# 64-row attention heads and a pipeline rotated by half a group in an attention-plus-FFN kernel

## The chip, the cores and the metric

The kernel runs on one core of one Trainium2 chip. The metric is the device time of one execution in microseconds (us), lower is better. A run has a state: slow when it is more than 1.5% above the fastest run of the same kernel, else fast; only fast runs are compared in ratios (a median is of all runs). The profile shows one execution. Its span is about 1.8 us shorter than the device time of the same execution (329.5 against 331.33 us), so profile spans and times are not mixed below.

Engines are named as the profile names them: PE is TensorE (matmul), PEld its weight loads, DVE VectorE, ACT ScalarE, POOL GpSimd, SP SyncE, which here only issues DMAs (SPq).

## The reference

There are 8 batches, 8 heads, 576 tokens and 64 columns per head. Every head gets two attentions that are added: a local one, in which token i sees the tokens with |i - j| < 4, and one over q, k and v averaged by fours (144 tokens), whose result is repeated four times. The sum becomes x with 4608 rows and 512 columns and goes through an FFN:

```python
def _attn_ref(q, k, v):                       # cut
    q_d = q.reshape(B, H, Sd, 4, D).mean(axis=3)      # k_d, v_d alike
    out_up = np.repeat(sm_attn(q_d, k_d, v_d), 4, axis=2)
    scores = np.where(np.abs(i - j) < 4, scale * q @ k.T, -1e9)
    return out_up + softmax(scores) @ v

def _moe_ref(x, w_in, w_out):
    h = x @ w_in                              # 512 -> 2048
    return (h * (1 / (1 + np.exp(-1.702 * h)))) @ w_out   # 2048 -> 512
```

## The kernel before

The FFN is cut into 9 groups of 512 tokens. A group is 64 large matmuls of the first product (16 blocks of 4, each followed by a silu on ACT) and 64 of the second. The attention of batch g + 1 is threaded into group g at fixed positions. A position below 16 counts blocks of the first product; from 16 on it counts single matmuls of the second.

```python
POS = [13, 16, 33, 42, 53, 62, 71]
# s_pe(0), s_act(0), scores of quad 1, values 0-1, values 2-3, transposes 0-1, 2-3

def prep_1(name, b, qd):                    # DVE: q or k of four heads, transposed
    store, dst = {"k": (kf, kT), "q": (qf, qT)}[name]
    tt = work.tile([128, S, 2], BF16, ...)
    nc.vector.transpose(out=..., in_=store[b, qd]...)   # pairs of bf16 moved as one fp32
    dst[b, qd] = tt

def scores(b, qd, barred=False):            # local scores of a quad of heads
    sp = [ps_tile(), ps_tile()]             # two of three PSUM tiles in rotation
    for i in range(5):
        for a in range(2):                  # even and odd columns of the head
            for par in range(2):
                for r in range(4):
                    rows = slice(32 * r, 32 * r + 32)
                    nc.tensor.matmul(sp[r // 2][...],
                        lhsT=kT[b, qd][rows, k0 : k0 + 64, a],
                        rhs=qT[b, qd][rows, q0 : q0 + 60, a],
                        start=(a == 0), stop=(a == 1),
                        tile_position=(32 * r, 64 * par))      # 80 matmuls
    return sp
# scores_d (pooled): the same way, 24 matmuls; pool_qk makes its operands on POOL

    for g in range(n_groups):               # cut
        ...
        elif b < B:                         # b = g + 1
            load_v4(b)                      # six DMAs on SP
            prep_qk(b, 0); pool_qk(b, 0)
            load_qk(b + 1, 0); load_qk(b + 1, 1)     # POOL's queue
            prep_v(b, nc.gpsimd)
            load_v(b + 1)                   # ten DMAs on SP
            prep_qk(b, 1); pool_qk(b, 1)
            prep_v4(b, nc.gpsimd)
```

The transpose moves pairs of bf16 numbers (in the trace one instruction of 128x576 f32, 1.24 us, the next 1.09 us later), so the 64 columns of a head lie on 32 partitions, with two columns behind each other on each. A head therefore takes two accumulating matmuls of 32 rows for every block of scores.

The softmax here doesn't subtract the row's maximum and nothing guards it: scores larger than these inputs give would overflow.

## Time and profile before

| | before |
|---|---|
| time, median of 3 | 329.24 us (328.62 to 329.56) |
| span of the profile | 329.5 us |
| TensorE busy | 308.0 us (93%) |
| groups 1 to 6, each with the attention of one batch | 33.4 to 35.1 us |
| groups 7 and 8, FFN alone | 27.6 and 31.4 us |

These lines are from the page of the kernel before: busy time of each engine (share of the span, instructions), and the shares of the chain that ended last, by engine.

```profile
PE 308.0 (93%) x4987; PEld 157.9 (48%) x5043; DVE 130.2 (40%) x215; ACT 184.1 (56%) x322; POOL 138.9 (42%) x168
...
PE 87%; issue 4%; SPq 3%; ACT 2%; DVE 2%; DMA 1%; DVEq 0%; ACTq 0%
```

TensorE is the limit: it is nearly always busy, and its work is 87% of the chain.

The next lines are the windows view, one line for a group, cut where the first large matmul of each group starts: groups 1, 2, 3, 6 and 7.

```profile
core 0: us, PE busy (x) PEld busy (x) DVE busy (x) ACT busy (x) POOL busy (x), PEclk, DMA share, GB/s
67.08:102.18 35.10, 33.30 (x594) 17.04 (x600) 17.43 (x27) 21.73 (x39) 17.52 (x19) 1.00 0.74 161
102.18:135.89 33.71, 32.80 (x594) 16.91 (x600) 16.34 (x25) 20.95 (x36) 17.52 (x19) 1.00 0.68 142
135.89:169.42 33.53, 32.63 (x594) 16.88 (x600) 16.33 (x25) 20.95 (x36) 17.53 (x19) 1.00 0.68 143
237.13:270.53 33.40, 32.50 (x595) 16.75 (x601) 14.99 (x25) 20.95 (x36) 15.25 (x15) 1.00 0.28 69
270.53:298.15 27.62, 27.51 (x127) 12.50 (x128) 0.52 (x2) 11.94 (x20) 0.00 (x0) 1.00 0.10 39
```

Group 7 has no attention: 27.62 us are 128 large matmuls. The attention of a batch costs TensorE the rest, 33.40 - 27.62 = 5.8 us. PEclk, the mean granted clock of TensorE, is 1.00 in every group. DVE works about half of a group, POOL too.

One block of scores stands like this in the timeline of TensorE (start, time until the end of the last one, line, names, shapes, count):

```profile
147.21 0.84 PE L351 MATMUL pa<-qT,kT 32*64 32x60 bf16 x80
147.85 0.59 PE L370 MATMUL pa<-qdT,kdT 32*64 32x144 bf16 x24
148.38 2.76 PE L618 MATMUL pm<-xT,w_in_bf 128*128 128x512 bf16 x11
```

The 80 local matmuls take 0.64 us until the pooled ones start, 8 ns each. So it is mostly their number that costs, and the change halves it.

### The profile page before, as it was taken

The numbers are of one execution on the slowest core, as the hardware profiler recorded it, in microseconds if no ns is written. First come the engines' busy times: TensorE is split into PE (matmuls) and PEld (weight loads), VectorE is DVE, ScalarE is ACT, GpSimd is POOL, SyncE is SP. The second block draws the span as 40 slices with busy tenths as digits, with TensorE's granted clock in tenths as the row PEclk, the third lists the DMA queues.
The fourth block names the chain that finished last, engine by engine and source line by source line (L and its number), as shares of the span: only waits on it lengthen the run. The fifth ranks groups of instructions, "written<-read, shape, count | busy, mean of one in ns | idle before, by whom it ended". The sixth has DMA issues, their size and how long they took to land.

```text
span 329.5 us, 11220 instructions
## 1 busy us (share of the span) xinstructions
PE 308.0 (93%) x4987; PEld 157.9 (48%) x5043; DVE 130.2 (40%) x215; ACT 184.1 (56%) x322; POOL 138.9 (42%) x168
## 2 busy tenths in 40 slices
PE   8767999789999999999999999998999999999995
PEld 3444455445554455455544555455444544444444
DVE  4870512770468036802771277225730560000000
ACT  2552773375936683667367746674566646415611
POOL 7890844049603970298029901990098000000000
PEclk9997999999999999999999999999999999999999
DMA  7999979999814991398339922993180110011011
GB/s 126 184 188 208 171 151 183 196 210 236 191 39 132 205 207 39 116 193 171 102 100 200 200 83 86 196 195 105 40 172 2 60 41 32 2 72 56 2 62 65
DMA packets 63552, 41.36 MB, mean 126 GB/s; under 512 B 44048, under 2 KB 54416, under 8 KB 63504
## 3 DMA queue, kind: packets, MB, share of 16 engines
q1 hardware_dynamic: 55056, 26.95, 35.8%
q0 software_dynamic: 8304, 13.63, 23.9%
q8 instruction: 39, 0.64, 0.9%
q14 instruction: 9, 0.07, 0.1%
q10 hardware_dynamic: 144, 0.07, 0.1%
HBM read 44.83 MB, written 9.44 MB: 165 GB/s over the span
## 4 chain that ended last, share of the span: by engine, by line
PE 87%; issue 4%; SPq 3%; ACT 2%; DVE 2%; DMA 1%; DVEq 0%; ACTq 0%
PE pm L618 35%; PE pm L674 33%; PE pa L351 3%; SPq L214 3%; PE pa L618 2%; PE pa L431 2%; PE pa L409 2%; PE pa L370 2%; PE pa L458 2%; PE pa L674 2%; DMA vf<-in_v_dram 1%; PE pm L689 1%; PE pa L484 1%; ACT vd L321 0%; PE pa L312 0%
## 5 line engine op out<-in xcount | busy, mean ns | idle before, releaser
L618 PE MATMUL pm<-xT,w_in_bf 128*128 128x512 bf16 x528 | 120.3, 380 | 1.4 <-DVE xT L561 0.7
L674 PE MATMUL pm<-w_out_bf,gT 128*128 128x512 bf16 x493 | 114.1, 379 | 5.4 <-issue 5.2
L629 ACT ACTIVATE gT<-pm 128x512 bf16<-128x512 f32 x136 | 81.0, 598 | 45.2 <-PE pm L618 45.2
L618 PEld LDWEIGHTS <-w_in_bf 128*128 128x128 bf16 x576 | 55.8, 98 | 68.4 <-issue 2.5
L674 PEld LDWEIGHTS <-gT 128*128 128x128 bf16 x560 | 51.7, 98 | 59.5 <-issue 0.2
L276 POOL TENSOR_TENSOR pq<-kT 128x576 f32<-128x576 bf16 x16 | 18.5, 1157 | 105.0 <-DVE kT L260 96.1
L395 DVE TENSOR_TENSOR es<-es,mask 128x600 bf16<-128x600 bf16 x28 | 20.6, 749 | 92.0 <-ACT es L381 91.2
L659 ACT ACTIVATE osb<-pm 128x512 f32<-128x512 f32 (+2 forms) x35 | 20.7, 592 | 40.2 <-PE pm L674 36.1
L534 ACT COPY od<-pa 128x384 f32<-128x384 f32 (+1 forms) x56 | 18.4, 412 | 32.4 <-DVE y L444 18.7
L444 DVE TENSOR_TENSOR y<-pa,rc 128x896 bf16<-128x896 f32 x32 | 34.9, 1092 | 1.1
L555 DVE TENSOR_TENSOR xT<-pa,od 128x570 bf16<-128x570 f32 x28 | 21.1, 753 | 12.0 <-ACT od L534 11.9
L381 ACT ACTIVATE es<-pa 128x600 bf16<-128x600 f32 x32 | 19.8, 668 | 7.0 <-PE pa L351 6.8
L297 POOL TENSOR_TENSOR v<-v 112x512 f32<-112x512 f32 x18 | 22.8, 1265 | 0.0
L661 DVE TENSOR_SCALAR osb<-pm 128x128 f32<-128x128 f32 x1 | 0.3, 292 | 55.3 <-ACT osb L659 55.3
L260 DVE STREAM_TRANSPOSE kT<-kb 128x576 f32<-128x576 f32 x16 | 20.0, 1249 | 2.0 <-DMA kb<-in_k_dram 2.0
L260 DVE STREAM_TRANSPOSE qT<-qb 128x576 f32<-128x576 f32 x16 | 19.8, 1239 | 0.9 <-DMA qb<-in_q_dram 0.7
L276 POOL TENSOR_TENSOR pq<-qT 128x576 f32<-128x576 bf16 x16 | 18.4, 1148 | 0.0
L291 POOL CAST vb<-vf 128x2560 bf16<-128x2560 f32 (+1 forms) x11 | 17.6, 1618 | 0.0
L442 DVE RECIPROCAL rc<-pa 128x14 f32<-128x14 f32 x32 | 7.7, 240 | 21.7 <-PE pa L431 21.7
L351 PE MATMUL pa<-qT,kT 32*64 32x60 bf16 x1280 | 14.0, 203 | 1.5 <-issue 1.5
L351 PEld LDWEIGHTS <-kT 32*64 32x64 bf16 x1280 | 11.8, 104 | 6.7 <-issue 5.5
L300 POOL TENSOR_TENSOR vd<-v 112x256 bf16<-112x256 f32 x18 | 13.7, 759 | 1.4
(90 smaller groups left out, 247.0 us busy)
## 6 DMA issues: line engine op xcount, KB each, us to landing
vf<-in_v_dram SPq DMA_DIRECT2D x80, 128.0 KB, 4.7
out_dram<-osb SPq DMA_DIRECT2D x35, 256.0 KB, 2.1
v<-in_v_dram SPq DMA_DIRECT2D x36, 192.0 KB, 6.1
kb<-in_k_dram POOLq DMA_DIRECT2D x16, 288.0 KB, 6.8
qb<-in_q_dram POOLq DMA_DIRECT2D x16, 288.0 KB, 7.1
w_out_bf<-in_moe_w_out_dram POOLq DMA_DIRECT2D x4, 512.0 KB, 12.1
w_in_bf<-in_moe_w_in_dram POOLq DMA_DIRECT2D x2, 512.0 KB, 5.7
w_in_bf<-in_moe_w_in_dram POOLq DMA_DIRECT2D x1, 1024.0 KB, 10.7
```

The source lines that it names most:

```text
L260: nc.vector.transpose(out=t32.rearrange("p (i c) -> p c i", c=18), in_=store[b, qd].bitcast(FP32).rearrange("p (c d) -> p c d", c=18),)
L276: nc.gpsimd.tensor_tensor(out=t1, in0=sv[:, :, 0:2, :], in1=sv[:, :, 2:4, :], op=ALU.add)
L297: eng.tensor_tensor(out=t1[0:112], in0=x[:, :, 0:2, :], in1=x[:, :, 2:4, :], op=ALU.add)
L351: nc.tensor.matmul(sp[r // 2][64 * par : 64 * par + 64, r % 2, 60 * i : 60 * i + 60], lhsT=kT[b, qd][rows, k0 : k0 + 64, a], rhs=qT[b, qd] ...
L381: nc.scalar.activation(out=es[2 * qd + u][:, :, 0:300], in_=sp[u][:, :, 0:300], func=AF.Exp, scale=inv_sqrt_d,)
L395: nc.vector.tensor_tensor(out=ev, in0=ev, in1=mask, op=ALU.mult)
L444: nc.vector.tensor_tensor(out=y, in0=ov[:, :, :, 0:D], in1=rc.to_broadcast([128, 2, 7, D]), op=ALU.mult,)
L555: eng.tensor_tensor(out=sub(xT[hp], t0 + 3, (57, 2), (114, 5), (1, 57)), in0=sub(x, 3, (509, 2), (57, 5), (1, 57)), in1=sub(od, 3, (57, 2) ...
L618: nc.tensor.matmul(acc, lhsT=w_in_bf[:, dmc, ffc * 128 : (ffc + 1) * 128], rhs=xT[dmc][:, g * TG : g * TG + TG], start=(dmc == 0), stop=(d ...
L629: nc.scalar.activation(out=gT[:, ffc, :], in_=acc, func=AF.Silu, scale=GELU_SCALE)
L659: eng.activation(out=osb, in_=ap, func=AF.Copy, scale=1.0 / GELU_SCALE)
L674: nc.tensor.matmul(ops[t], lhsT=gT[:, ffc, t * 128 : (t + 1) * 128], rhs=w_out_bf[:, ffc, :], start=(ffc == 0), stop=(ffc == n_ffc - 1),)
```

## The change

There are two parts.

1. **64-row heads from batch 3 on** (`ROWS64 = 3`). A second transpose of the same data and four small SBUF-to-SBUF DMAs for each of q and k, shifted by one element, put all 64 columns of a head on 64 partitions. A quad then needs 40 + 12 matmuls for its scores in place of 80 + 24.
2. **A rotated timetable.** The new preparation takes longer, so from group 3 on the scores of batch g + 2 are made at the end of group g, and its values at the start of group g + 1. Groups 1 and 2 are the way there: group 1 holds the two scores blocks of batch 2 and the first one of batch 3; group 2 the second one of batch 3 and both of batch 4.

```diff
     def prep_1(name, b, qd):
+        n = 2 if b >= ROWS64 else 1
+        tt = work.tile([128, 2, S, 2], BF16, ...)
+        for x in range(n):
+            nc.vector.transpose(out=<tt[:, x]>, in_=<store[b, qd]>)
+        if n == 2:
+            for x in range(2):
+                f = tt[:, x].rearrange("p t a -> p (t a)")
+                for r in range(2):
+                    src = 64 * r + 32 * x
+                    to = 64 * r + 32 * (1 - x)
+                    nc.sync.dma_start(
+                        out=f[to : to + 32, 0 : 2 * S - 1], in_=f[src : src + 32, 1 : 2 * S])
     def scores(b, qd, barred=False):
         sp = [ps_tile(), ps_tile()]
+        if b >= ROWS64:                    # 5 x 2 x 2 x 2 = 40 matmuls
+            ... rows = slice(64 * u, 64 * u + 64) ... start=True, stop=True
+            return sp
 ... scores_d alike (12 matmuls), pool_qk alike
-    POS = [13, 16, 33, 42, 53, 62, 71]
+    at(1, 0, ...)    # as before: q, k and values of batch 2
+    at(1, 13, s_pe, 2, 0)
+    at(1, 16, s_act, 2, 0, True, False)
+    at(1, 16, prep_qk, 3, 0)
+    at(1, 18, s_all, 2, 1, False, False)      # was position 33
+    at(1, 32, avn, 2, P01)
+    at(1, 40, avn, 2, P23)
+    at(1, 48, tr, 2, P01)
+    at(1, 56, tr, 2, P23)
+    at(1, 57, load_v, 4)
+    at(1, 66, s_all, 3, 0, False, True)
+    at(2, 0, prep_qk, 3, 1)
+    at(2, 0, pool_qk, 3, 1)
+    at(2, 0, prep_qk, 4, 0)
+    at(2, 12, s_pe, 3, 1)
+    at(2, 25, avn, 3, P01)
+    at(2, 57, s_all, 4, 0, False, False)
+    at(2, 67, s_all, 4, 1, False, True)
 ... (mask, pooling, loads and value sums of both groups cut)
+    for g in range(3, B - 1):               # b = g + 1, c = g + 2, cut
+        at(g, 0, prep_qk, c, 0); at(g, 8, prep_qk, c, 1)
+        at(g, 6, avn, b, P01); at(g, 11, avn, b, P23)
+        at(g, 16, tr, b, P01); at(g, 25, tr, b, P23)
+        at(g, 40, s_all, c, 0, True, False)
+        at(g, 56, s_all, c, 1, False, True)
+        at(g, 57, load_v, c + 1)
```

Quad n of batch b is called (b,n) from here on.

## The prediction

> **What bounds it.** TensorE. The page has PE 93% busy and PE work as 87% of the chain that ended last. By the timeline of PE, groups 3 to 6 take 33.53, 33.39, 34.32 and 33.39 us; groups 7 and 8, without attention, 27.63 and 27.74 us (128 matmuls started every 0.216 us). So attention costs about 5.8 us of PE per group and PE hardly waits: the one gap is 0.62 us in group 5. Starts of neighbouring large matmuls give the blocks: scores of a head quad 1.26 us in the first half of a group, 1.47 us in the second (80 local matmuls in 0.64 to 0.84 us, 24 pooled in about 0.5); values of two head pairs 0.92; transposes 0.66.
>
> **Removed.** For batches 3 to 7 a quad needs 40 + 12 score matmuls instead of 80 + 24.[...] But in this trace small matmuls are bound by their number: 32-row ones come every 8 ns, 64-row ones (20 local value matmuls in 0.18 us) every 9 ns. Estimate from values (80 matmuls, 0.92 us) and transposes (52, 0.66): 0.18 us fixed plus 9.3 ns each. New scores: 0.18 + 40 x 9.3 ns + 12 x about 17 ns = 0.75 us. Gain 0.5 to 0.7 us, ten times: about 5.5 us.
>
> **Added, off the path.** A second stream transpose for each k and q (1.09 us apart, 20 more), four small SBUF copies each (80 DMAs). DVE is 40% busy, 16 us of a 33 us group; group 2 gets twelve transposes (13 us). Rotation gives this time: from group 3 on q/k of the batch ahead are needed 22 us into the group and should be ready after about 13 (copies issue behind ten value loads that hold the SP queue 10.4 us). I expect no stall over 0.5 us there.
>
> **New waits.**
> - Group 1: scores (2,1) move from position 33 to 18, two large matmuls after position 16, and use the same PSUM tiles as (2,0), by the instruction order. These are freed by the local exponentials, which follow the last silu (ends 15.24 us into the group), a 1.28 us table load and 1.23 us of exp: 17.8 us. PE arrives at 15.0 us: **2.7 us idle**[...].
> - Group 1: the four transposes of (3,0) stand ahead of the mask of (2,1) and the normalisations on DVE: about 1 us more at values P23 and at scores (3,0).
> - Group 2: 0.5 to 1 us (pooled scores (3,1) waiting for copies and POOL; tiles released by merges).
>
> **Sum.** -5.5, -0.6 (group 5's gap, perhaps), +2.7, +1.0, +0.7: about -1.7 us. By group: 1 takes 38 us (it also gets a third scores block), 2 about 34, 3 to 5 about 32.4, 6 about 30.8, 7 and 8 unchanged.
>
> Predicted: 327.5 us, range 324.0 to 330.5. Chances: faster by over 2% 0.08, within 2% 0.88, slower by over 2% 0.04.
>
> **Right if** the timeline shows new scores at 0.7 to 0.85 us, DVE transposes and DMA packets up without PE waiting for them in groups 3 to 6, and PE idle about 2.7 us before scores (2,1), released by ACT's local exp.
>
> **Wrong if** 64-row matmuls come slower than 9 ns apart (gain halves), the copies land late behind value loads and stall scores in every group (slower), the exponentials of (2,0) run earlier than I think (about 324), or group 2's DVE load stalls PE by several us.

## The result and the profile after

| | median, us | lowest and highest | runs |
|---|---|---|---|
| before | 329.4 | 328.62 to 330.18 | 4 |
| after | 340.58 | 339.08 to 340.88 | 4 |

The results are correct. The ratio is 1.033 with a 95% interval from 1.0291 to 1.037: the changed kernel is **slower**, by 3%. Here and below a ratio is the mean time of one kernel's fast runs over that of the other's of the same rounds, so it is not quite the ratio of the medians that are quoted. Below, each set of runs has its own runs of the kernel before on the same chip; their medians lie between 329.4 and 331.8 us.

The lines of the page that answer to those of before, with the granted clock in 40 slices (tenths) and one line of the DMA issues (count, size, us from issue to landing):

```profile
PE 310.1 (92%) x4470; PEld 155.3 (46%) x4523; DVE 158.5 (47%) x237; ACT 182.2 (54%) x320; POOL 142.1 (42%) x168
...
PEclk9985999999699989999999999999999999999999
...
PE 79%; DMA 5%; issue 5%; DVE 4%; ACT 3%; SPq 2%; POOL 2%; POOLq 0%; DVEq 0%; ACTq 0%
...
kT<-kT SPq DMA_DIRECT2D x40, 71.9 KB, 2.1
```

TensorE runs 517 matmuls fewer, yet is busy for longer. A slice is 8.4 us. In the row of the clock, slice 11 (84 to 93 us) has a 6 and slice 15 (118 to 126 us) an 8; the low digits of slices 3 and 4 belong to the start. In the chain, TensorE fell from 87% to 79%, and DMA, DVE, ACT and POOL came in.

The windows of groups 1, 2, 3, 6 and 7 after the change:

```profile
68.16:109.05 40.89, 36.51 (x646) 18.37 (x652) 23.94 (x36) 23.69 (x42) 31.37 (x33) 0.92 0.95 201
109.05:149.88 40.83, 34.93 (x541) 17.42 (x548) 25.10 (x35) 22.94 (x40) 18.29 (x21) 0.96 0.78 165
149.88:182.48 32.60, 31.96 (x491) 15.84 (x496) 25.74 (x30) 21.42 (x37) 20.83 (x23) 1.00 0.80 175
247.48:278.28 30.80, 30.43 (x389) 14.79 (x393) 8.67 (x16) 14.45 (x28) 1.12 (x2) 1.00 0.10 37
278.28:305.90 27.62, 27.52 (x127) 12.54 (x128) 0.00 (x0) 11.94 (x20) 0.00 (x0) 1.00 0.10 39
```

Group by group, from the same view:

| group | 0 | 1 | 2 | 3 | 4 | 5 | 6 | 7 | 8 |
|---|---|---|---|---|---|---|---|---|---|
| before | 67.08 | 35.10 | 33.71 | 33.53 | 33.40 | 34.31 | 33.40 | 27.62 | 31.35 |
| predicted for after | unchanged | 38 | 34 | 32.4 | 32.4 | 32.4 | 30.8 | unchanged | unchanged |
| after | 68.16 | 40.89 | 40.83 | 32.60 | 32.46 | 32.54 | 30.80 | 27.62 | 31.40 |
| after less before | +1.08 | +5.79 | +7.12 | -0.93 | -0.94 | -1.77 | -2.60 | 0.00 | +0.05 |

The steady part of the pipeline came out as intended. Groups 1 and 2, in which it is turned round, take back twice as much. Group 0 is the same program in both; in the profile after, TensorE spent 10.2 us of the start at half clock against 3.4 us before, which the change does not touch. Over all kernels, which are the same program up to there, group 0 ended at 66.6 to 69.5 us, so the +1.08 us is within what executions of it differ by. Only this one execution is taken apart below; the other three of the changed kernel had a mean clock of 0.973 to 0.979 against 0.968 here, so the clock's share of the loss differs from one to the next.

### What 64 rows gave

This is the first scores block of group 3 in TensorE's timeline after the change.

```profile
172.34 0.52 PE L381 MATMUL pa<-qT,kT 64*64 64x60 bf16 x40
172.72 0.38 PE L416 MATMUL pa<-qdT,kdP 64*64 64x144 bf16 x12
173.26 3.40 PE L727 MATMUL pm<-w_out_bf,gT 128*128 128x512 bf16 x15 [0.16 <-issue]
```

40 matmuls in 0.38 us are 9.5 ns each. What the block costs is read from the groups: group 6 has values and transposes alone (30.80 us), a clean group of the new form 32.40 us, so two blocks cost 1.60 us, 0.80 us each. Two 32-row blocks cost 33.40 - 30.80 = 2.60 us. The gain is 1.0 us for a batch, 5 us in all.

### Group 1: a wait, and then the clock

This is TensorE's timeline of the kernel after around the second scores block of batch 2 (in brackets, the idle time of the engine before the line and what ended it):

```profile
87.10 0.26 PE L398 MATMUL pa<-qT,kT 32*64 32x60 bf16 x2 [2.23 <-ACT es L441]
87.67 0.92 PE L398 MATMUL pa<-qT,kT 32*64 32x60 bf16 x78 [0.31 <-ACT es L441]
89.81 5.03 PE L727 MATMUL pm<-w_out_bf,gT 128*128 128x512 bf16 x13 [0.33 <-issue]
```

ACT's timeline of the same kernel, just ahead of it:

```profile
84.47 0.60 ACT L682 ACTIVATE gT<-pm 128x512 bf16<-128x512 f32 x1 [0.27 <-PE pm L671]
85.09 1.28 ACT L646 ACT_TABLE_LOAD   x1
86.38 1.23 ACT L441 ACTIVATE es<-pa 128x600 bf16<-128x600 f32 x2
```

At position 18 TensorE wants the PSUM tiles of the block before. They come free only with the exponentials, which stand behind the last silu and a table load of 1.28 us. The wait is 2.23 + 0.31 = 2.54 us. After it, 13 large matmuls take 5.03 us, 0.39 us each on average in place of 0.216: TensorE runs at half clock.

In this trace half clock starts at 15.45, 25.69, 87.13 and 124.68 us (and once more 1 us before the end). These four times lie 3, 18 and 11 steps of 3.413 us apart, and each of the four stretches is one or two steps long. So the trace can be cut into windows of one step. These are two neighbouring ones from each of the two groups; the clock of the kernel after is in the third column from the end.

```profile
83.72:87.13 3.41, 1.18 (x8) 0.42 (x7) 0.05 (x1) 3.12 (x5) 3.25 (x4) 1.00 1.05 191
87.13:90.54 3.41, 2.77 (x106) 2.00 (x107) 3.32 (x4) 3.06 (x5) 2.40 (x3) 0.50 0.89 193
121.27:124.68 3.41, 0.97 (x51) 0.68 (x43) 1.84 (x2) 0.00 (x0) 2.47 (x3) 1.00 0.39 90
124.68:128.09 3.41, 3.19 (x18) 1.20 (x9) 2.67 (x3) 0.60 (x1) 1.65 (x2) 0.50 0.45 108
```

In the window that ends at 87.13 us TensorE was busy for 1.18 us of 3.41, or 35%, and the next window was granted half the clock. The clock stayed there for two windows, 6.83 us. In group 2 the same happened once.

### Group 2: the copies are issued late

The timeline of SP's queue around the start of group 2 (109.05 us) in the kernel after:

```profile
101.35 13.24 SPq L218 DMA_DIRECT2D vf<-in_v_dram  x10
114.69 1.04 SPq L717 DMA_DIRECT2D out_dram<-osb  x2
115.83 2.50 SPq L276 DMA_DIRECT2D kT<-kT  x4
118.42 2.44 SPq L276 DMA_DIRECT2D qT<-qT  x4
```

DVE's timeline of the same kernel and time:

```profile
107.89 2.33 DVE L266 STREAM_TRANSPOSE kT<-kb 128x576 f32<-128x576 f32 x2
110.07 2.31 DVE L266 STREAM_TRANSPOSE qT<-qb 128x576 f32<-128x576 f32 x2
```

The transposes of (3,1) are done at 112.4 us. The eight copies that complete its q and k could have been issued then, but the queue is held by the ten value loads of batch 4 until 114.6 us and by two stores until 115.7. The copies themselves take 0.61 us each to issue, 4.94 us for eight. The last is issued at 120.9 us. TensorE waits for it, then for POOL, which can only pool q once it is complete. Its timeline there:

```profile
120.61 0.18 PE L381 MATMUL pa<-qT,kT 64*64 64x60 bf16 x1 [1.03 <-DMA qT<-qT]
124.45 0.41 PE L416 MATMUL pa<-qdT,kdP 64*64 64x144 bf16 x12 [1.71 <-POOL qdT L301]
```

With three smaller waits and one of 0.71 us before the values, TensorE idles 4.5 us in these waits, and 3.41 us of the group run at half clock.

### The profile page after: what moved, and what is told of

Its sections match the earlier page's. It is cut to its first block, busy times and chain, and to the rows that moved or that the text cites. A ratio compares the mean times of both kernels' runs of the same rounds, so it can differ in the third digit from the quotient of the medians.

```text
span 337.3 us, 10429 instructions
## 1 busy us (share of the span) xinstructions
PE 310.1 (92%) x4470; PEld 155.3 (46%) x4523; DVE 158.5 (47%) x237; ACT 182.2 (54%) x320; POOL 142.1 (42%) x168
## 4 chain that ended last, share of the span: by engine, by line
PE 79%; DMA 5%; issue 5%; DVE 4%; ACT 3%; SPq 2%; POOL 2%; POOLq 0%; DVEq 0%; ACTq 0%
PE pm L671 34%; PE pm L727 29%; PE pa L671 2%; DMA qb<-in_q_dram 2%; SPq L276 2%; DMA qT<-qT 2%; PE pa L469 2%; PE pa L491 2%; PE pa L727 2%; DMA v<-in_v_dram 1%; PE pa L518 1%; PE pa L381 1%; PE pm L742 1%; DVE qT L266 1%; PE pa L398 1%
## 5 line engine op out<-in xcount | busy, mean ns | idle before, releaser
L671 PE MATMUL pm<-xT,w_in_bf 128*128 128x512 bf16 x529 | 123.3, 384 | 1.6 <-DVE xT L621 0.7
L727 PE MATMUL pm<-w_out_bf,gT 128*128 128x512 bf16 x495 | 116.5, 384 | 4.5 <-issue 3.2
L727 PEld LDWEIGHTS <-gT 128*128 128x128 bf16 x560 | 52.6, 99 | 62.4 <-issue 3.6
L455 DVE TENSOR_TENSOR es<-es,mask 128x600 bf16<-128x600 bf16 x28 | 27.6, 1013 | 44.1 <-ACT es L441 43.6
L504 DVE TENSOR_TENSOR y<-pa,rc 128x896 bf16<-128x896 f32 x32 | 34.9, 1092 | 1.1
L266 DVE STREAM_TRANSPOSE kT<-kb 128x576 f32<-128x576 f32 x26 | 30.8, 1242 | 9.5 <-DMA kT<-kT 6.1
L266 DVE STREAM_TRANSPOSE qT<-qb 128x576 f32<-128x576 f32 x26 | 30.6, 1237 | 0.9 <-DMA qb<-in_q_dram 0.9
L328 POOL TENSOR_TENSOR v<-v 112x512 f32<-112x512 f32 x18 | 24.4, 1358 | 7.5 <-DMA v<-in_v_dram 7.5
L292 POOL TENSOR_TENSOR pq<-qT 128x576 f32<-128x576 bf16 x10 | 11.5, 1152 | 7.0 <-DMA qT<-qT 5.0
L447 ACT ACTIVATE ed<-pa 128x864 bf16<-128x864 f32 x15 | 13.5, 897 | 0.0
## 6 DMA issues: line engine op xcount, KB each, us to landing
kT<-kT SPq DMA_DIRECT2D x40, 71.9 KB, 2.1
qT<-qT SPq DMA_DIRECT2D x40, 71.9 KB, 2.0
```

The costliest lines, as they stand in the source:

```text
L266: nc.vector.transpose(out=t32.rearrange("p (i c) -> p c i", c=18), in_=store[b, qd].bitcast(FP32).rearrange("p (c d) -> p c d", c=18),)
L292: nc.gpsimd.tensor_tensor(out=t1, in0=sv[:, :, 0:2], in1=sv[:, :, 2:4], op=ALU.add)
L328: eng.tensor_tensor(out=t1[0:112], in0=x[:, :, 0:2, :], in1=x[:, :, 2:4, :], op=ALU.add)
L455: nc.vector.tensor_tensor(out=ev, in0=ev, in1=mask, op=ALU.mult)
L504: nc.vector.tensor_tensor(out=y, in0=ov[:, :, :, 0:D], in1=rc.to_broadcast([128, 2, 7, D]), op=ALU.mult,)
L671: nc.tensor.matmul(acc, lhsT=w_in_bf[:, dmc, ffc * 128 : (ffc + 1) * 128], rhs=xT[dmc][:, g * TG : g * TG + TG], start=(dmc == 0), stop=(d ...
```

## The experiments

Four explanations are weighed here; the expectations were written before and may name theirs in other words. Late copies: the copies behind the value loads on SP's queue cause the loss of group 2. Early scores: the early place of the scores of (2,1) causes the loss of group 1, about half of it by the clock. Rotation (a rival): the new timetable itself costs in groups 1 and 2, whatever the rows. No need (another rival): the 64-row preparation fits into the old timetable, and the rotation is not needed. Every experiment gives correct results. All edits are against the changed kernel, unless another is named. Each kernel was profiled once, so its groups are those of one execution. Slow runs are in no ratio: there was one of four in rows64_values_first, two of six in rows64_best and one of six in rows64_best_later; those of rows64_spread and of the kernel before are named below.

The groups of the experiments, from the windows view (us; group 6 is 30.8 us in every rotated kernel, groups 7 and 8 as before):

| kernel | 1 | 2 | 1 + 2 | 3 | 4 | 5 |
|---|---|---|---|---|---|---|
| before | 35.10 | 33.71 | 68.8 | 33.53 | 33.40 | 34.31 |
| after | 40.89 | 40.83 | 81.7 | 32.60 | 32.46 | 32.54 |
| values_later | 38.58 | 39.38 | 78.0 | 33.89 | 32.40 | 32.39 |
| scores_later | 37.30 | 47.18 | 84.5 | 32.73 | 32.60 | 32.52 |
| fill_wait | 39.13 | 46.12 | 85.3 | 32.70 | 32.40 | 32.57 |
| rows32 | 38.78 | 41.02 | 79.8 | 33.50 | 33.46 | 33.59 |
| copies_on_pool | 39.59 | 42.25 | 81.8 | 32.75 | 32.40 | 32.58 |
| rotation_mended | 37.91 | 35.39 | 73.3 | 34.58 | 32.52 | 33.68 |
| rotation_fewer_copies | 37.91 | 39.55 | 77.5 | 32.72 | 32.53 | 32.40 |
| rotation_fewer_late | 37.91 | 37.50 | 75.4 | 32.56 | 32.40 | 32.40 |
| rotation_mixed | 37.28 | 35.38 | 72.7 | 32.56 | 32.53 | 32.48 |
| rotation_mixed_late | 37.02 | 34.85 | 71.9 | 32.56 | 32.40 | 32.47 |

### One cause taken away at a time

These four were run together; the kernel before had a median of 331.8 us (330.78 to 335.1, 7 runs) beside them.

**values_later**: the value loads of batch 4 go behind the copies of (3,1).

```diff
-    at(1, 57, load_v, 4)
     at(2, 0, prep_qk, 3, 1)
     at(2, 0, pool_qk, 3, 1)
+    at(2, 0, load_v, 4)
     at(2, 0, prep_qk, 4, 0)
```

> One edit: the value loads of batch 4, which in the changed kernel are issued in group 1 and hold the SP queue for 13.2 us, are issued in group 2, behind the copies of (3,1). Same transposes, same copies. Queue theory: the copies of (3,1) are issued as soon as their transposes end (about 112 us in the changed kernel's trace, in place of 115.8 to 120.9), the wait of PE before scores (3,1) falls from about 5 us to under 0.5 us, PE keeps full clock in group 2, and group 2 falls from 40.8 us to 34 to 36 us (copies of (4,0) now stand behind the value loads, so a small wait there is possible); total about 5 us less than the changed kernel, 335 us. Rival (twelve transposes make VectorE too slow): the transposes are as many, so group 2 stays near 40 us.

It took 334.86 us; the ratio is 1.0098 (1.000 to 1.0195), so about 1% of loss is left where the changed kernel had 3.3%. The waits for copies before (3,1) are gone, but one of 2.34 us for POOL's pooled q is left there, and 3.41 us at half clock follow as before, so group 2 falls only by 1.5 us. Group 1 is 2.3 us shorter although its wait is as long as before (2.24 + 0.34 us). The windows view of this run around the wait:

```profile
82.09:85.50 3.41, 1.50 (x7) 0.59 (x6) 0.00 (x0) 2.87 (x4) 3.25 (x4) 1.00 1.09 205
85.50:88.91 3.41, 2.52 (x109) 1.79 (x110) 3.01 (x4) 3.13 (x6) 2.76 (x3) 1.00 0.77 173
```

The windows are counted back in steps of 3.41 us from the half clock of group 2, which starts at 119.64 us; the boundary at 85.50 us is ten steps before it. The same wait falls here across this boundary. The two windows are 44% and 74% busy, and the clock stays at 1.00. So half clock cost group 1 of the changed kernel about 40.89 - 38.58 = 2.3 us. That the place of the windows decided whether it struck is my reading of these two executions.

**scores_later**: the scores of (2,1) come 12 positions later, and all that follows in group 1 too.

```diff
-    at(1, 18, s_all, 2, 1, False, False)
+    at(1, 30, s_all, 2, 1, False, False)
     # values 32, 40 -> 41, 48; transposes 48, 56 -> 55, 62
     # load_v(4) 57 -> 63; scores (3,0) 66 -> 71
```

> One edit: in group 1 the scores (2,1) go from position 18 to 30, and values, transposes, the value loads of batch 4 and scores (3,0) follow at later positions. Theory of the PSUM tiles: the 2.6 us for which PE waits on the exponentials of (2,0) go, and with them the half clock that follows (3 us): group 1 falls from 39.2 to about 34.5 us, clock 1.0 in it; group 2 may change by 1 us either way. Total about 336 us. Rival (group 1 is long because VectorE runs the transposes of (3,0) ahead of the masks): the wait only moves to the values, and group 1 stays over 37 us.

It took 342.06 us; the ratio is 1.0283 (1.0213 to 1.0352). Group 1 fell to 37.30 us, as early scores would have it, but group 2 rose to 47.18 us. The timeline of SP's queue in this run:

```profile
103.44 12.67 SPq L218 DMA_DIRECT2D vf<-in_v_dram  x10
...
117.35 2.49 SPq L276 DMA_DIRECT2D kT<-kT  x4
```

TensorE's timeline in this run:

```profile
122.11 0.23 PE L381 MATMUL pa<-qT,kT 64*64 64x60 bf16 x1 [5.82 <-DMA qT<-qT]
```

TensorE arrived early at (3,1), and the copies came no earlier, as the queue was still held by the value loads. The time won in group 1 was spent waiting in group 2, and 10.24 us of half clock followed.

**fill_wait**: twelve large matmuls of zeros are put into the wait of group 1, to keep TensorE busy.

```diff
+    at(1, 18, dummies, 12)
     at(1, 18, s_all, 2, 1, False, False)
```

> One addition: twelve dummy 128x512 matmuls (2.6 us at full clock) into the idle PSUM tile in front of scores (2,1), so that PE is busy while it waits; the exponentials come no earlier. Theory of the clock (the half clock from 87 to 94 us follows from the idle time before it): clock stays 1.0 through group 1, and group 1 falls from 39.2 to 36 to 37 us; total about 338 us. Rival (the low clock there is not caused by this wait): group 1 stays near 39 us or grows.

It took 342.33 us; the ratio is 1.030 (1.024 to 1.0359). The dummies fill the wait, so nothing of it is saved. The clock of group 1 is now 1.00, and the group is 1.8 us shorter than in the changed kernel: this confirms the cost of the clock. Group 2 took it back again (46.12 us: waits of 4.05, 2.24 and 1.59 us and 10.24 us at half clock). It is the same as in scores_later: what group 1 gives goes into the wait for the copies.

**rows32**: the rotated timetable with 32-row heads for every batch, so without second transposes and copies.

```diff
-    ROWS64 = 3
+    ROWS64 = 8
```

> One constant: the 64-row form is turned off, the rotation and all positions stay. No copies, half the transposes. Queue theory: scores (3,1) wait no longer for copies, group 2 is about 35 us (with 1.3 us for each scores block), group 1 stays near 39.5 us with its wait and half clock, groups 3 to 5 are about 33.5 us in place of 32.5, group 6 30.8. Total about 338 us. If the rotation itself were the loss, group 2 would stay near 40 us.

It took 341.16 us; the ratio is 1.0264 (1.0189 to 1.0339). If late copies were all, group 2 would have come down to its work, which with three blocks at 1.30 us is 34.7 us by the sums below. It takes 41.02 us without a single copy, 3.41 us of them at half clock. It has other waits, the longest ones before values; in the timeline of TensorE:

```profile
127.44 0.35 PE L469 MATMUL pa<-vb,es 64*64 64x65 bf16 x20 [0.68 <-DVE es L455]
129.09 0.36 PE L469 MATMUL pa<-vb,es 64*64 64x65 bf16 x20 [1.12 <-DVE y L504]
```

So the rival of the rotation holds in part: the copies are the wait that ends last in group 2 of the changed kernel, but others lie hidden beside them and come out when the copies are gone. Groups 3 to 5 are at 33.5 us, which gives the price of 32 rows in the rotated form: 0.9 to 1.1 us for a batch.

### Another queue, and no rotation

These four were run together; the kernel before had a median of 330.06 us (329.05 to 333.1, 7 runs).

**copies_on_pool**: the copies are issued from POOL's queue.

```diff
-                    nc.sync.dma_start(
+                    nc.gpsimd.dma_start(
```

> One edit: the 80 copies are issued from the POOL queue instead of the SP queue, so no value load stands ahead of them; transposes, positions and rotation stay. Queue theory: PE's wait before scores (3,1) falls from about 5 us to 2 us or less (the pooling of (3,1) still follows the copies in POOL's order), and group 2 falls from 40.8 us to 36 to 38 us, unless the half clock strikes there; group 1 keeps its 2.6 us wait (38.6 us without, 41 us with the half clock). Total about 335 us. Rival (the waits come from the number of transposes or from the rotation's order on other engines): group 2 stays at 40 us or more, as it did with 32 rows.

It took 337.73 us; the ratio is 1.0183 (1.0099 to 1.0267). Group 2 is no better (42.25 us; 1.71, 0.36, 0.40 and 1.79 us of waits for copies and pooled q, and 6.8 us at half clock). This misses the expectation (36 to 38 us). The copies of (3,1) were issued 4.8 to 8.7 us into the group, in place of 6.8 to 11.8, yet POOL waited for those of k until 117.8 us and for those of q until 120.2 us, as those copies took 4.8 and 5.5 us to land (medians) while the value loads ran. So the place in SP's queue is not all that holds the copies. Issued from POOL's queue, a copy takes 3.9 to 4.3 us to land (medians) against 2.0 to 2.1 us from SP in the changed kernel, and its issue takes 0.50 us from POOL, on which the pooled q waits. Moving the queue alone does not help.

**rows64_old_times**: 64 rows from batch 3 on in the old timetable and the old order of loads, except that the second quad's transposes and copies go ahead of the next value loads.

```diff
-    <all plans of groups 1 to 6>
+    # POS = 13, 16, 33, 42, 53, 62, 71 in every group, loads as before the change
```

> The 64-row form alone, without rotation: the positions of the kernel before in groups 1 to 6, copies of both quads issued ahead of the next value loads, value loads of v4 still first in the group. Theory (the rotation's transition in groups 1 and 2 is the whole loss, the 64-row form a gain of about 1 us per batch): groups 1 and 2 as before (35.1 and about 33 us), groups 2 to 6 at 32.5 to 34 us with a wait of up to 1.5 us at scores (b,0), which come 11.2 us into the group while their copies and pooling end after 12 to 13 us. Total 325 to 331 us. Rival (the 64-row form needs the rotation, since its preparation is too long for the old positions): each of groups 2 to 6 waits over 3 us and the total is over 338 us.

It took 377.4 us; the ratio is 1.142 (1.1323 to 1.1517). That the rotation is not needed falls here: groups 2 to 6 take 39.4 to 44.3 us. The pooled scores of group 2 in TensorE's timeline:

```profile
117.82 0.38 PE L416 MATMUL pa<-qdT,kdP 64*64 64x144 bf16 x12 [2.52 <-POOL qdT L301]
```

The same group in the windows view (length, busy times, granted clock, DMA share, GB/s):

```profile
103.11:146.73 43.62, 37.60 (x498) 17.51 (x496) 19.94 (x29) 20.84 (x36) 18.34 (x19) 0.88 0.66 137
```

Each of groups 2 to 6 waits for the preparation and loses clock after it. In this order of work, the preparation needs the rotation.

**rows64_values_first**: no rotation; POOL casts and sums the values first, both quads are prepared at the start of the group, and all loads go behind the copies.

```diff
+        at(g, 0, prep_v, b, nc.gpsimd)
+        at(g, 0, prep_qk, b, 0)
+        at(g, 0, prep_qk, b, 1)
+        at(g, 0, prep_v4, b, nc.gpsimd)
+        at(g, 0, pool_qk, b, 0)
+        at(g, 0, load_qks, b + 1)      # then load_v, load_v4
+        at(g, 0, pool_qk, b, 1)
+        # old positions 13, 16, 33, 42, 53, 62, 71
```

> As rows64_old_times, but POOL does the value casts and sums of the batch at the start of the group, while the transposes and copies run, and value loads are issued behind the copies. Expected: POOL work ahead of the pooled keys ends 8.4 us into the group, copies of q land at about 9.7, pooling of (b,0) ends at 12, scores (b,0) begin at 11.2 and need the pooled ones at 11.6: waits under 1 us. Groups 2 to 6 take 32.3 to 33.3 us, clock 0.995, total 324 to 327 us, faster than both kernels. Rival as above: waits over 3 us in each group.

It took 339.1 us; the ratio is 1.0234 (1.0153 to 1.0314). The groups 2 to 6 fell to 33.6, 33.5, 34.9, 34.0 and 32.8 us, with waits of 0.9 to 1.4 us before the pooled scores of the second quad in groups 2 to 5. Group 1 rose to 39.8 us, with waits of 1.42 us for pooled q and of 1.90 us put down to issue (on these, see rows64_best), and 3.41 us at half clock. So most of the preparation can be hidden without rotation as well, if its order is changed; but groups 2 to 6 together are still no shorter than before (168.9 against 168.3 us).

**rows64_from_2**: the same with 64 rows from batch 2 on.

```diff
-    ROWS64 = 3
+    ROWS64 = 2
```

> As rows64_values_first, with the 64-row form from batch 2 on, so that group 1 takes it too. Expected: group 1 falls from 35.1 to about 34 us, total about 1 us under rows64_values_first, 323 to 326 us. If the loads of group 0 still fill the queues at the start of group 1 the copies land late there and group 1 gains nothing.

It took 337.94 us; the ratio is 1.0218 (1.015 to 1.0286). The batch more of 64 rows left group 1 at 39.3 us, where TensorE waits 1.91 and 1.37 us for pooled q.

### No rotation, in its best form

These two and rotation_mended were run together; the kernel before had a median of 331.05 us (328.45 to 333.15, 11 runs).

**rows64_best**: group 1 keeps the old order; in the others the pooling of both quads is put ahead of the q and k loads. **rows64_best_later** is the same with the second scores at position 36 and the first values at 44.

```diff
+            at(g, 0, pool_qk, b, 0)
+            at(g, 0, pool_qk, b, 1)
+            at(g, 0, load_qks, b + 1)   # then load_v, load_v4
```

> rows64_values_first mended at two places that its profile showed: group 1 keeps its old order (there the values ahead of the keys cost 4.7 us), and from group 2 on the pooling of (b,1) stands ahead of the next q/k loads, whose 1.2 MB delayed the landing of the last q copy from 2 to 6 us. No rotation, positions of the kernel before. Expected: group 1 35.1 us, groups 2 to 6 32.3 to 32.9 us with no wait over 0.5 us and full clock, 1.0 to 1.2 us less per group than before; total 324 us, 1.3 to 1.9% under the kernel before. Rival (the 64-row form's gain is always eaten by its preparation): 328 us or more.

> As rows64_best, with scores (b,1) at position 36 in place of 33 and the values at 44 and 54, to give copies and pooling of (b,1) 0.65 us more. If rows64_best still waits for the pooling, this is up to 0.6 us per group faster; if not, the same within 1 us, 324 us.

They took 337.3 us (ratio 1.0193, 1.0144 to 1.0242) and 339.77 us (1.0272, 1.0218 to 1.0327). No wait for POOL is left in groups 2 to 5 of the first, and still they take 34.4 to 35.7 us. The time is in one gap per group which the profile puts down to "issue", which is to nothing that it shows. In TensorE's timeline of rows64_best:

```profile
130.66 1.46 PE L727 MATMUL pm<-w_out_bf,gT 128*128 128x512 bf16 x6 [1.74 <-issue]
...
161.14 0.19 PE L469 MATMUL pa<-vb,es 64*64 64x65 bf16 x1 [2.10 <-issue]
```

By the packed trace, each of these gaps (groups 2 to 5) begins between 0.3 us before and 0.8 us after the start of a 16 KB transfer on the queue that the profile calls instruction, and ends 2.2 to 2.5 us after it; the DMA engines are fully busy at that time (from 126 to 134 us 90% or more in each slice of 0.2 us). A possible reading is that TensorE waits for its next instructions, which the loads hold up. A test was tried:

**rows64_spread**: rows64_best with q and k in one tile, four copies in place of eight for a quad, and the value loads moved to positions 42 and 64.

```diff
-                at(g, 0, load_v, b + 1)
-                at(g, 0, load_v4, b + 1)
+                at(g, 42, load_v, b + 1)
+                at(g, 64, load_v4, b + 1)
```

> rows64_best, with the copies merged as above and the value loads moved from the middle of the group (where q/k, v and v4 loads came together) to positions 42 and 64. rows64_best had in each of groups 2 to 5 a gap of 1.7 to 2.6 us 'issue' on PE[...], in stretches where the DMA engines are busy throughout. Theory (those gaps are PE waiting for its instructions behind the loads): with the loads apart the gaps shrink under 0.8 us, groups 2 to 5 fall from 34.4 to 35.7 us to 33 us, total 328 to 331 us. Rival (the gaps come with the 64-row form itself): they stay.

Three of its four runs were slow ones, the profiled one too, so it has no ratio; the one fast run took 340.35 us (the kernel before had a median of 330.92 us beside it). The gaps stayed (1.3 to 2.3 us in groups 1 to 5 of the profile). But the new position 42 put the value loads into the very stretch of the gaps, where the DMA engines were still busy (a share of 0.88 to 1.23), so this run does not decide. What the traces show speaks for the waiting: all 18 together have, from 60 us on, 39 gaps of over 0.5 us on TensorE that are put down to issue, that of 0.62 us in group 5 of the kernel before among them, and every one ends 2.2 to 3.0 us after the start of a 16 KB instruction transfer. This is agreement in time. No run shows that the loads are what makes the transfer late, and that stays open.

### The rotation, mended

**rotation_mended**: scores_later and values_later together, and the preparation of (3,1) moved from the start of group 2 to the end of group 1.

```diff
     <edits of scores_later>
-    at(1, 63, load_v, 4)
+    at(1, 63, prep_qk, 3, 1)
+    at(1, 63, pool_qk, 3, 1)
-    at(2, 0, prep_qk, 3, 1)
-    at(2, 0, pool_qk, 3, 1)
+    at(2, 0, load_v, 4)
     at(2, 0, prep_qk, 4, 0)
```

> The rotation kept, its waits in groups 1 and 2 attacked together: scores (2,1) at position 30 as in scores_later, transposes, copies and pooling of (3,1) moved from the start of group 2 to position 63 of group 1, and the value loads of batch 4 put behind those copies. Theory (the loss is these two waits and the half clock after them, not the rotation as such): group 1 36 to 37.5 us, group 2 34 to 36 us, no half clock after 70 us, groups 3 to 6 as in the changed kernel; total 326 to 330 us. Rival (a group with three scores blocks waits whatever the order): groups 1 and 2 together stay over 75 us, total over 333 us.

It took 331.48 us; the ratio is 1.0001 (0.9939 to 1.0063). With the three edits together the loss of 3% is gone. Groups 1 and 2 take 73.3 us in place of 81.7; their clock is 1.00. Group 3 now has waits of 0.51 us for value sums and 1.19 us for pooled q, group 5 one of 0.70 us.

The next two were run with rows64_spread; the kernel before had a median of 330.92 us (329.18 to 332.67, 11 runs).

**rotation_fewer_copies**: rotation_mended with k and q in one tile, so that one copy moves both: 4 in place of 8 for a quad. **rotation_fewer_late** also has the second scores of groups 3 to 5 at position 60 in place of 56.

```diff
+        kq[qd] = work.tile([128, 2, 2, S, 2], BF16, ...)      # k and q of a quad
+                    nc.sync.dma_start(
+                        out=f[to : to + 32, :, x, 0 : 2 * S - 1],
+                        in_=f[src : src + 32, :, x, 1 : 2 * S])
```

> rotation_mended, with k and q of a quad in one tile, so that one DMA copies both: 40 copies in place of 80, the same bytes. Theory (issue on the SP queue, 0.6 us per copy[...], still holds up the copies in groups 2 to 5 of rotation_mended, where 2 to 3 us of waits for pooling and late values are left): SP time per group falls by about 4 us, waits in groups 3 to 5 fall under 0.5 us each, total 1 to 3 us under rotation_mended, ratio 0.985 to 0.997. Rival (the DMA engines, not the issue, are the limit: same bytes, same landing): ratio as for rotation_mended, 1.00.

> As rotation_fewer_copies, with the second scores of groups 3 to 5 at position 60 in place of 56, 0.9 us later. If pooling of the second quad is still late, the waits before pooled scores in groups 3 to 5 (1.2 and 0.7 us in rotation_mended) go and the total falls by up to 1.5 us; if the exponentials and the table load then run into the next group's silu, group boundaries grow by as much.

They took 334.56 us (1.0109, 1.007 to 1.0149) and 333.81 us (1.0072, 1.0028 to 1.0115). Groups 3 to 5 are clean now at 32.4 to 32.7 us, where rotation_mended had 32.5 to 34.6; the changed kernel had 32.5 to 32.6 with eight copies too, so fewer issues are not shown to be needed for it. Up to group 2 the two are the same program, yet group 2 took 39.55 us in one, with 3.41 us at half clock, and 37.50 us in the other, with none: one profile can be 2 us off in such a group. But a joint copy must wait until q is transposed too, and where time is scarce, in group 2, that costs 2.34 and 1.80 us of waiting for the pooled q of (3,1).

The last two were run together; the kernel before had a median of 331.2 us (327.75 to 334.15, 11 runs, three of them slow).

**rotation_mixed**: rotation_fewer_late, but batch 3 keeps separate copies; joint ones from batch 4 on. **rotation_mixed_late** also has the values and transposes of groups 1 and 2 up to four positions later.

```diff
-        if b >= ROWS64:        # joint copies
+        if b > ROWS64:
+        if b == ROWS64:        # in prep_1: separate copies
     # rotation_mixed_late, group 1: 48 -> 52, 55 -> 58, 62 -> 65, 63 -> 66, 71 -> 72
     # group 2: 25 -> 28, 33 -> 36, 41 -> 43, 49 -> 50
```

> The best parts of the last runs: as rotation_fewer_late, but the copies of batch 3 stay one per tensor, so that k's go ahead while q is transposed (merged, they came 2 us too late in group 2); from batch 4 on one copy carries k and q. Expected: group 1 37.9 us, group 2 35.4 us as in rotation_mended, groups 3 to 5 32.5 us as in rotation_fewer_late, group 6 30.8: 3.3 us under rotation_mended, total about 328 us, ratio 0.987 to 0.995. If issue on the SP queue does not matter in group 2, group 2 stays at 37.5 us or more and the ratio at 1.00 or more.

> As rotation_mixed, with the values and transposes of groups 1 and 2 up to 4 positions later, where PE waited 1.1 us for the normalised values and 0.7 us for the exponentials. Expected: those two waits go, 0 to 1.5 us under rotation_mixed; copies of (3,1) stand behind one more store and may come 1 us later in group 2, which would take the gain back.

They took 329.96 us (ratio 0.9993, 0.9936 to 1.005) and 328.3 us (0.9952, 0.9887 to 1.0017). SP's queue in the timeline of rotation_mixed_late:

```profile
103.76 5.36 SPq L279 DMA_DIRECT2D kq<-kq  x8
...
109.88 9.62 SPq L218 DMA_DIRECT2D vf<-in_v_dram  x10
```

TensorE's timeline of the same run, at the scores of (3,1):

```profile
115.88 0.52 PE L394 MATMUL pa<-kq 64*64 64x60 bf16 x40
116.22 0.37 PE L429 MATMUL pa<-qdT,kdP 64*64 64x144 bf16 x12
```

The windows view of its groups 1 and 2:

```profile
67.70:104.72 37.02, 35.45 (x653) 17.79 (x652) 23.48 (x35) 22.97 (x42) 25.69 (x28) 1.00 0.88 190
104.72:139.57 34.85, 33.89 (x549) 16.68 (x548) 28.20 (x35) 23.60 (x40) 24.35 (x27) 1.00 1.01 224
```

The copies of (3,1) are issued before the value loads, 12 us ahead of their use; TensorE waits neither for them nor for the pooled q, and the clock is 1.00 in both groups. This is the best version that I found. Its fast runs are 0.5% shorter than those of the kernel before, with an interval that includes no difference. It is not shown to beat the kernel before.

## Why the prediction was wrong

I predicted 327.5 us, and the range up to 330.5 us did not hold the 340.58 us that were measured. Most of the prediction's steps held, and the two that failed lay in 82 us of the 340. Everything that I had listed under "Right if" was seen, for none of these signs looks at group 2 or at the clock; under "Wrong if" I had named copies behind value loads, but "in every group".

**What held.** TensorE is the limit. A 64-row block costs 0.80 us (0.75 predicted, 0.7 to 0.85 named as the sign), since these matmuls come every 9 to 10 ns, as 32-row ones do every 8, and there are half as many. The gain is 1.0 us for a batch (1.1 predicted); groups 3 to 5 take 32.5 us (32.4 predicted), group 6 30.8 us (30.8 predicted). The wait before (2,1) is 2.54 us (2.7 predicted), and the local exponentials end it, as predicted.

**Failed: "Group 2: 0.5 to 1 us (pooled scores (3,1) waiting for copies and POOL; tiles released by merges)".** The place and the mechanism were right, and the size was wrong. Group 2 takes 7.1 us more than before. I had named the value loads that hold SP's queue, and had counted them only for groups 3 to 6, where there is plenty of time. I had not put the queue's times in a row for group 2: the value loads of batch 4 are issued at the end of group 1 and hold the queue until 114.6 us (13.24 us; 10.4 assumed), and the issue of eight copies takes 4.9 us, which I had costed at nothing. The first copy was issued 3.4 us after the transposes were done, the last one 8.5 us after. values_later removes the copies' waits; scores_later and fill_wait show that whatever time TensorE gains before this point is lost at it.

**Failed: +2.7 us for the wait of group 1, with nothing for the clock.** That the clock stays at 1.00 through this wait was an assumption of mine that no trace showed. In the trace of the changed kernel a wait of 2.54 us was enough: the window around it was 35% busy, and 6.83 us of half clock followed, at a cost of 1.8 us (fill_wait) to 2.3 us (values_later).

**Not seen where it was predicted: "about 1 us more at values P23".** The changed kernel has no such wait, and it is not that half clock hides it: values_later and fill_wait have the same positions in group 1 at a clock of 1.00 and do not have it either. It comes only where the scores of (2,1) are at position 30: 0.88 us before those values in scores_later, 1.11 us in rotation_mended, 0.91 us in rotation_mixed, ended by the normalisation on DVE.

**The sum.** Group 1: 35.10 before, 0.80 for the third scores block, 2.54 of waits and about 2.3 of clock are 40.7 us, where 40.89 was measured. Group 2: 27.62 of FFN, three blocks at 0.80, and values with transposes 30.80 - 27.62 = 3.18 are 33.2 us of work; 4.5 us of waits, and at most half of the 3.41 us at half clock, 1.7 us, lead to 39.4; the remaining 1.4 us are not assigned. Against the prediction by groups this is +2.9 us in group 1, +6.8 in group 2, +0.4 in groups 3 to 5 and +1.1 in group 0 (the start, which differs between executions), together 11.2 us; the profiled run took 339.08 us, which is 11.6 us above the prediction.

**What the rivals said.** That the rotation is not needed fell in rows64_old_times; with the order of preparation changed too the loss is smaller (1.9% in rows64_best), but the intervals of all versions without rotation that have one lie above 1.4%. That the rotation itself costs in groups 1 and 2, without copies, is right in part: rows32 takes 41.02 us for group 2, against 34.7 us of work. So no single edit mends the kernel. It took three: the scores of (2,1) later, the preparation of (3,1) earlier, the value loads behind its copies (rotation_mended, 1.0001). I ran no two of these three without the third, nor the earlier preparation alone, so the share of each is not known.

**Where the gain goes in the best version.** In the profile of rotation_mixed_late groups 3 to 6 are 6.4 us shorter than before, and groups 1 and 2 are 3.1 us longer (71.9 against 68.8 us). Of these 3.1 us, 0.6 are work: before, the two groups held four blocks of 1.30 us; now they hold two of 1.30 and four of 0.80. The other 2.5 us are waits and gaps, such as 0.40 us for a merge ahead of the pooled scores of (3,0) and 0.54 us for the output of group 1. What is left of the 5 us, and of a gap of 0.6 us in group 5 of the kernel before, is 3.3 us by the groups, about 1%; the runs give 0.5% with an interval of about 0.65% to each side, which is too wide to confirm it.

**Open.** Why the instruction transfers come too late in the kernels without rotation, if they are what their gaps wait for; the 1.4 us of group 2; and why the multiplication by the mask on DVE takes 1013 ns on average after the change and 749 before (the page's lines of groups). In these two traces each of them takes 448 to 474 ns where POOL is idle, and 471 to 4780 ns where POOL is busy for more than half of it; before, 14 of 28 met a busy POOL, after it 23. No run tested whether POOL is the cause.

## What to carry to other kernels

When a change adds DMAs, cost the issue of each one on its queue and draw up that queue's timetable for the tightest stretch, not for the steady state: there copies that landed in 2.0 to 2.1 us (medians) were issued up to 8.5 us late, as they stood behind loads that nobody needed yet and behind each other. A stretch in which a pipeline is turned round deserves its own sum, with every wait listed, as here removing one wait only showed the next: in scores_later group 1 fell by 3.6 us and group 2 rose by 6.4 us. On TensorE a wait can cost nearly twice its length: 2.54 us cost 1.8 to 2.3 us more in half clock where it left one window of 3.41 us 35% busy, and 2.58 us in values_later cost no clock where they fell across two (44% and 74%).

## What the traces showed of the hardware

- The clock of TensorE. Waits of 2.23 + 0.31 us that left a window of 3.41 us 35% busy were followed by half clock. 14 of the 18 traces were cut into such windows. In them, from 40 us on, full-clock windows that were at most 41% busy were followed by half clock in 18 of 19 cases (the exception, in rows64_best, was 40% busy), those at 42 to 44% went both ways, and none that was at least 52% busy was. At the start this does not hold: there a window of the changed kernel that was 60% busy (22.28 to 25.69 us) was followed by half clock. Half clock came in lengths of 3.41, 6.83 and 10.24 us, at 0.50.
- Small matmuls started 8 ns (32 rows, 80 in 0.64 us) to 9.5 ns (64 rows, 40 in 0.38 us) apart here, so half as many for the same scores are worth 1.0 us for a batch.
- Small copies. Those issued from POOL's queue took 3.9 to 4.3 us to landing (medians) beside other loads. Those from SP took 2.0 to 2.1 us in the changed kernel, and in rotation_mixed_late 4.3 us, or 3.1 us for the joint ones. The issue of one copy of 32 rows held SP's queue for 0.61 us in the changed kernel's quickest fours (2.43 to 2.50 us) and up to 0.92 us in its slowest (3.68 us). A joint one, of twice the bytes, took 0.65 to 1.03 us in rotation_fewer_copies (2.58 us for four, 8.26 us for eight). Ten value loads of 128 KB that were issued into busy DMA engines (a share of 1.14) took 13.24 us. This time delayed the copies in group 2.
- rows64_best has gaps of 1.7 to 2.6 us on TensorE, each ending 2.2 to 2.5 us after the start of an instruction transfer of 16 KB. What they wait for is open.
